# A balanced-experts router and its FFN: each full expert's list, rows, weights and matmuls moved into the rounds that follow

## The chip, the cores and the metric

One core of one Trainium2 chip. The time is the device time of one execution in microseconds (us); lower is better. The kernel before took 676.96 us (median of 4 runs beside the changed kernel; 678.58 in the 3 runs that the prediction had).

Engines: PE is TensorE's matmuls, PEld its weight loads, DVE VectorE, ACT ScalarE, POOL GpSimd, SP SyncE (it issues DMA).

## The reference, cut to what matters

Linear attention with gates over 4 x 8 x 768 x 48 gives 3072 tokens of 384 numbers. A router then sends every token to one of 8 experts, each with room for exactly 384:

```python
logits = x @ w_gate
order = np.argsort(-logits.flatten())
for idx in order:                       # greedy, best logit first
    tok, e = idx // E, idx % E
    if assigned[tok] >= 0 or counts[e] >= cap: continue
    assigned[tok] = e; counts[e] += 1
for e in range(E):
    h = np.maximum(x[assigned == e] @ w1[e], 0.0)     # 384x384 by 384x1024
    out[assigned == e] = h @ w2[e]                    # 384x1024 by 1024x384
```

## The kernel before

Both kernels do the greedy loop in seven rounds and a last choice. In a round each free token names its best open expert; a search over the key's bits (two searches of four steps) finds the level at which the first expert fills up; tokens above it are assigned for good. So each round fills at least one expert. One search step of the kernel before:

```python
for shift in (12, 8, 4, 0):
    level = steps * unit + base                                 # DVE, 15 levels
    above = cand >= level                                       # DVE, 128 x 24 x 15
    for c in range(NT):                                         # PE, 24 small matmuls
        nc.tensor.matmul(out=cnt[0:NTH, 0:E], lhsT=above[:, c, :], rhs=choice[:, :, c], ...)
    fills = cnt >= wanted; filled = max(fills)                  # DVE
    nc.tensor.matmul(out=digit[:, 0:1], lhsT=ones[0:NTH, :], rhs=filled[0:NTH, :], ...)
    base = digit * unit + base                                  # DVE
```

(Shortened: operand details are left out.) Every line needs the one before it. After the last round one list of all tokens in expert order is made, and then, expert by expert, rows are gathered, turned, and multiplied:

```python
xTs = {0: gather(0)}
for e in range(E):
    if e + 1 < E:
        xTs[e + 1] = gather(e + 1)          # indirect DMA, 3 x 3 transposes, DVE copy
    ffn(e, xTs.pop(e), *weights[e])         # 24 + 24 fp32 products of 128 x 128 by 128 x 384
    if len(weights) < E:
        weights.append(load_weights(len(weights)))   # the first three loaded during attention
```

## Time and profile before

| stage of the profiled run (span 675.2 us) | from, to (us) | what limits it |
|---|---|---|
| attention | 0 to 181 | PE (busy 161 us) and the engines around it |
| router, seven rounds of 29.3 us | 181 to 388 | a chain DVE, PE, DVE, PE; PE busy 28% |
| last choice, list, first gather | 388 to 412 | DVE (busy 11.7 of the first 14 us), then POOL and DMA (POOL busy 6.8 of the last 10) |
| eight FFNs of 31.9 us | 412 to 669 | PE, without a gap (busy 256 of 257 us from 412 to 669) |
| last write | 669 to 675 | |

The lines behind the table are in the prediction. Read it as two stages with opposite limits, one after the other: the router leaves PE mostly idle (28% busy), the FFN leaves DVE, ACT and POOL mostly idle (11 to 15% busy).

### The profile page before, as it was taken

How to read it: one execution, taken by the hardware profiler on the slowest of the kernel's cores; microseconds unless marked ns; L12 is line 12 of the kernel's file. 1: busy time of each engine (PE TensorE's matmuls, PEld its weight loads, DVE VectorE, ACT ScalarE, POOL GpSimd, SP SyncE). 2: the span in 40 equal slices, each digit the busy share in tenths (PEclk: the TensorE clock that was granted, in tenths of full speed). 3: DMA queues.
4: the chain of work that ended last, by engine and by line, in shares of the span. 5: the costliest groups of instructions: out<-in, count | busy, mean ns of one | idle time of the engine just before them, and what ended most of it. 6: DMA issues, size and time to landing. Idle time of an engine off the chain costs nothing.

```text
span 675.2 us, 13443 instructions
## 1 busy us (share of the span) xinstructions
PE 481.7 (71%) x5769; PEld 332.5 (49%) x5769; DVE 274.6 (41%) x827; ACT 101.9 (15%) x245; POOL 104.9 (16%) x173
## 2 busy tenths in 40 slices
PE   2999999999332323223232307999999999999996
PEld 1788878888321312212131204565656565665553
DVE  3566656556457476675757662010101010201010
ACT  3355545442000000000000000010101010101100
POOL 5134343232000000000000006020212121010101
PEclk9999999998755555555555556999999999999999
DMA  8888889891000000000000005242424343300000
GB/s 169 172 185 171 184 172 255 245 345 64 30 2 0 2 0 1 1 1 1 1 1 1 1 0 140 106 151 106 151 105 153 116 141 116 106 23 12 36 0 35
DMA packets 118353, 59.14 MB, mean 88 GB/s; under 512 B 101648, under 2 KB 112912, under 8 KB 118288
## 3 DMA queue, kind: packets, MB, share of 16 engines
q1 hardware_dynamic: 111760, 44.06, 25.3%
q0 software_dynamic: 3072, 9.44, 3.9%
q10 hardware_dynamic: 3456, 4.72, 1.9%
q8 instruction: 47, 0.77, 0.5%
q14 instruction: 18, 0.15, 0.1%
HBM read 48.77 MB, written 9.44 MB: 86 GB/s over the span
## 4 chain that ended last, share of the span: by engine, by line
PE 29%; DVE 22%; issue 19%; POOL 2%; DMA 0%; POOLq 0%; DVEq 0%
PE H L663 10%; PE O L674 9%; PE cnt L507 7%; DVE above L499 4%; POOL out_dram L678 2%; DVE level L496 2%; PE digit L515 1%; DVE best L461 1%; DVE fills L510 1%; DVE filled L513 1%; DVE base L522 1%; PE Xe L651 1%; POOL xe L646 1%; DVE chosen L481 1%; DVE rank_incl L530 1%
## 5 line engine op out<-in xcount | busy, mean ns | idle before, releaser
L507 PE MATMUL cnt<-choice,above 128*15 128x8 bf16 x1344 | 44.5, 175 | 119.2 <-DVE above L499 119.2
L663 PE MATMUL H<-xeT,w 128*128 128x384 f32 x384 | 126.2, 489 | 0.0
L674 PE MATMUL O<-w,hT 128*128 128x384 f32 x384 | 125.2, 486 | 0.0
L507 PEld LDWEIGHTS <-above 128*15 128x15 bf16 x1344 | 38.6, 91 | 146.1 <-DVE above L499 133.7
L674 PEld LDWEIGHTS O<-w,hT 128*128 128x128 f32 x384 | 73.1, 190 | 50.7
L663 PEld LDWEIGHTS H<-xeT,w 128*128 128x128 f32 x384 | 73.2, 192 | 49.4 <-issue 0.9
L668 DVE TENSOR_SCALAR hT<-H 128x384 f32<-128x384 f32 x32 | 17.9, 558 | 120.8 <-PE H L663 105.3
L666 ACT ACTIVATE hT<-H 128x384 f32<-128x384 f32 x32 | 15.7, 490 | 339.7 <-PE H L663 339.7
L646 POOL DMA_INDIRECT xe<-xd,token x24 | 23.3, 971 | 259.2 <-issue 242.2
L678 POOL DMA_INDIRECT out_dram<-o,token x24 | 23.5, 981 | 198.5 <-ACT o L677 197.3
L653 DVE COPY xeT<-Xe 128x384 f32<-128x384 f32 x24 | 12.3, 553 | 100.4 <-PE Xe L651 98.4
L225 DVE COPY_PREDICATED am<-mask,A 128x512 f32<-128x512 int32 x48 | 32.4, 729 | 34.8 <-PE A L220 34.8
L151 PE MATMUL L<-g,wcum 128*128 128x384 f32 x48 | 24.3, 593 | 10.0 <-POOL ramp_i L402 10.0
L677 ACT COPY o<-O 128x384 f32<-128x384 f32 x24 | 11.5, 478 | 128.1 <-PE O L674 128.1
L499 DVE TENSOR_TENSOR above<-hi,level 128x360 bf16<-128x360 f32 x56 | 29.8, 532 | 1.2
L175 POOL TENSOR_TENSOR kg<-k,ek 128x384 f32<-128x384 f32 x24 | 25.6, 1066 | 27.2 <-ACT ek L163 21.4
L510 DVE TENSOR_TENSOR fills<-cnt,wanted 15x8 f32<-15x8 f32 x56 | 8.6, 153 | 50.0 <-PE cnt L507 50.0
L237 PE MATMUL Y<-v,am 128*64 128x48 f32 x768 | 27.8, 226 | 0.0
L220 PE MATMUL A<-qT,kT 48*64 48x128 f32 x768 | 27.7, 285 | 0.0
L237 PEld LDWEIGHTS Y<-v,am 128*64 128x64 f32 x768 | 24.7, 139 | 3.9 <-issue 3.7
L515 PE MATMUL digit<-filled,ones 15*128 15x1 bf16 x56 | 9.0, 161 | 24.1 <-DVE filled L513 24.1
L160 DVE TENSOR_SCALAR dl<-L 128x384 f32<-128x384 f32 x24 | 13.4, 558 | 27.7 <-PE L L155 27.7
(155 smaller groups left out, 553.3 us busy)
## 6 DMA issues: line engine op xcount, KB each, us to landing
w<-in_moe_w_dram SPq DMA_DIRECT2D x16, 1536.0 KB, 8.2
f<-in_f_logit_dram SPq DMA_DIRECT2D x24, 192.0 KB, 4.2
q<-in_q_dram SPq DMA_DIRECT2D x24, 192.0 KB, 3.9
k<-in_k_dram SPq DMA_DIRECT2D x24, 192.0 KB, 4.0
v<-in_v_dram SPq DMA_DIRECT2D x24, 192.0 KB, 4.2
xd<-x ACTq DMA_DIRECT2D x24, 192.0 KB, 3.6
xe<-xd,token POOLq DMA_INDIRECT x24
out_dram<-o,token POOLq DMA_INDIRECT x24
```

Of the source, the lines that this page charges most:

```text
L151: nc.tensor.matmul(out=Lv, lhsT=wcum[:], rhs=g[:, :, 0:DH], start=True, stop=True)
L175: nc.gpsimd.tensor_tensor(out=kg[:, :, 0:DH], in0=G["k"][:], in1=ek[:], op=ALU.mult)
L220: nc.tensor.matmul(out=A[par][HC * j:HC * j + HC, 128 * hp:128 * hp + 128], lhsT=G["kT"][rows, hp, HC * j:HC * j + HC], rhs=G["qT"][rows, ...
L225: nc.vector.copy_predicated(am[:, par], mask[:].unsqueeze(1).to_broadcast((128, HP, 128)), A[par][:].rearrange("s (a t) -> s a t", t=128))
L237: nc.tensor.matmul(out=Y[par][HC * j:HC * j + HC, DH * hp:DH * hp + DH], lhsT=G["am"][:, par, hp, HC * j:HC * j + HC], rhs=G["v"][:, 2 * h ...
L499: nc.vector.tensor_tensor(out=above[:], in0=cand[:].rearrange("p (c o) -> p c o", o=1).to_broadcast((128, NT, NTH)), in1=level[:].rearrang ...
L507: nc.tensor.matmul(out=cnt[0:NTH, 0:E], lhsT=above[:, c, :], rhs=choice[:, :, c], start=(c == 0), stop=(c == NT - 1))
L646: nc.gpsimd.indirect_dma_start(out=xe[:], out_offset=None, in_=xd[:, :], in_offset=bass.IndirectOffsetOnAxis(ap=token[:, t:t + 1], axis=0))
L663: nc.tensor.matmul(out=Hp[:, 0:CAP], lhsT=w1[:, d, 128 * ft:128 * ft + 128], rhs=xT[:, d, :], start=(d == 0), stop=(d == DC - 1))
L668: nc.vector.tensor_scalar(out=hT[:, ft, :], in0=Hp[:, 0:CAP], scalar1=0.0, scalar2=None, op0=ALU.max)
L674: nc.tensor.matmul(out=O[:, 0:D], lhsT=hT[:, ft, 128 * i:128 * i + 128], rhs=w2[:, ft, :], start=(ft == 0), stop=(ft == FC - 1))
L678: nc.gpsimd.indirect_dma_start(out=outs[t][:, :], out_offset=bass.IndirectOffsetOnAxis(ap=token[:, t:t + 1], axis=0), in_=o[:], in_offset= ...
```

## The change

Its intent is to run the two stages at once. An expert that a round has filled will never change, so its list, its row gather, its weight load and its FFN can start, and its products ("pieces" below: one fp32 product, or the three transposes that turn one block of rows) can be laid into PE's waits in the later rounds. Two queues hold the work, and the router takes from them at fixed places. The core of the diff (cuts marked):

```diff
     def search(choice, over, between):
         for shift in (12, 8, 4, 0):
             above = rt([NT, NTH], "above", BF16)
             tt(above[:], col(over[:], NTH), row(steps[shift][:], NTH), ALU.is_ge)
+            some(pe_work, between[0])          # pieces before cnt
             r = bank("cnt", "r")
             for c in range(NT):
                 nc.tensor.matmul(out=r[0:NTH, 0:E], lhsT=above[:, c, :], rhs=choice[:, c, :], ...)
+            some(dve_work, 2)                  # two bits of the list
             ...fills, filled...
+            some(pe_work, between[1])          # pieces before the digit
             nc.tensor.matmul(out=r[:, E:E + 1], lhsT=units[shift][0:NTH, :], ...)
+            some(dve_work, 1)
             new = rt([NT], "over")
             tt(new[:], over[:], r[:, E:E + 1].to_broadcast((128, NT)), ALU.add)
     ...
     def assign(choice, over, between):
         ...three matmuls of sums...
+        some(pe_work, between[2])
         ...
+    for rnd in range(E - 1):
+        choice, best = choices()
+        high, low = keys(best)
+        over = search(choice, high, (0, 0) if rnd < 2 else (2, 1))
+        stt(over[:], over[:], 65536.0, low[:], ALU.mult, ALU.add)
+        over = search(choice, over, (2, 1))
+        some(dve_work, len(dve_work))
+        assign(choice, over, (0, 0, 10))
+        dve_work.extend(expert_list())         # its last bit extends pe_work by ffn(L)
+        if rnd in (0, E - 2):
+            some(dve_work, len(dve_work))
+    ...last choice, last list...
+    some(pe_work, len(pe_work))                # what is left: the tail
```

Besides, the search keeps over (the key less the level) in place of a level, the logits are stored with the experts innermost, keys are made for the best logit only, ScalarE takes all evacuations of the FFN, and no weights are loaded during attention, because which expert comes first isn't known then.

## The prediction

> **What bounds the kernel now.** I read the windows first, then the page's slices, then the timeline of one search step. By TensorE's clock and the engines' work the span falls into attention (0 to 181 us), router (181 to 388), list and first gather (388 to 412), expert FFNs (412 to 669) and a 6 us end. Windows over the last three stages (length, busy time of each engine, granted clock, DMA share, GB/s):
>
> ```profile
> 181.00:388.00 207.00, 58.79 (x1421) 46.42 (x1422) 132.60 (x523) 0.00 (x0) 0.00 (x0) 0.50 0.00 1
> 388.00:412.00 24.00, 5.46 (x40) 3.49 (x40) 14.12 (x30) 0.00 (x0) 6.84 (x7) 0.50 0.17 45
> 412.00:669.00 257.00, 256.08 (x828) 153.13 (x827) 27.89 (x52) 27.12 (x56) 39.03 (x41) 0.99 0.27 93
> ```
>
> No engine is full in the router: PE 28%, DVE 64%, ACT, POOL and DMA idle. It is latency, a chain that goes back and forth. In the FFN stage PE is full. The change wants to lay the second stage's matmuls into the first's holes. One search step of the timeline (start, length, engine, line):
>
> ```profile
> 230.09 0.79 PE L507 MATMUL cnt<-choice,above 128*15 128x8 bf16 x24 [1.09 <-DVE above L499]
> 230.81 0.10 PEld L515 LDWEIGHTS <-ones 15*128 15x128 bf16 x1
> 230.92 0.15 DVE L510 TENSOR_TENSOR fills<-cnt,wanted 15x8 f32<-15x8 f32 x1 [0.89 <-PE cnt L507]
> 231.11 0.15 DVE L513 TENSOR_REDUCE filled<-fills 15x1 bf16<-15x8 f32 x1
> 231.32 0.16 PE L515 MATMUL digit<-filled,ones 15*128 15x1 bf16 x1 [0.43 <-DVE filled L513]
> 231.51 0.16 DVE L522 SCALAR_TENSOR_TENSOR base<-digit,base 128x1 f32<-128x1 f32 x1 [0.25 <-PE digit L515]
> 231.71 0.23 DVE L496 TENSOR_SCALAR level<-steps,base 128x15 f32<-128x15 f32 x1
> 231.97 0.53 DVE L499 TENSOR_TENSOR above<-hi,level 128x360 bf16<-128x360 f32 x1
> ```
>
> A step takes 2.47 us (the next cnt starts at 232.56), and PE has two holes in it: 0.43 us before digit and 1.09 before cnt. Eight steps make 19.8 of a round; successive choices start 29.3 us apart (chain of waits: best at 271.05, 300.34, 329.61), so 9.5 us are the assignment and the new choice, nearly all DVE. From the page, what is to fill the holes, and the clock:
>
> ```profile
> L663 PE MATMUL H<-xeT,w 128*128 128x384 f32 x384 | 126.2, 489 | 0.0
> L674 PE MATMUL O<-w,hT 128*128 128x384 f32 x384 | 125.2, 486 | 0.0
> ...
> PEclk9999999998755555555555556999999999999999
> ```
>
> The loops give 8 x 24 products of each kind, the page counts 384: an fp32 product is two passes, each 126.2/384 = 0.33 us of PE. The chain of waits shows 48 of them in 15.48 us. So one of the change's pieces (one product) costs **0.645 us** at full clock, and a piece that turns rows (three transposes) 0.33 (9 in 0.98 us). An expert is 3 x 0.33 + 48 x 0.645 = 31.9 us. A piece is bigger than the hole before digit, and two (1.29) are bigger than the hole before cnt. This decides the case.
>
> [...] 0.50 in the router, 0.99 in the FFN, with the rise about 2.5 us after dense matmuls begin at 413.5. But the windows show 0.50 at 150 to 155 us with PE busy throughout, after a stretch of tiny matmuls and a 0.70 us gap, so "busy" in the trace isn't all that counts. [...] the trace has 617 for the old layout with experts outermost and 358 for count, whose inner axis is contiguous. The new layout makes the inner axis contiguous, so I take 0.36.
>
> **The change part by part.**
>
> *Cheaper steps.* level (0.23 + 0.03 gap) goes; base on one column becomes over on 24 (+0.02). A step with no pieces: 2.47 - 0.26 + 0.02 = 2.23 us.
>
> *Cheaper choice.* The two products for high and low and their reduces go (2 x 0.27 + 2 x 0.53 by start-to-start); six key operations on 24 elements come (four before the search, 0.8). Choices: four operations at 0.39, two reduces at 0.39, one of 0.2: 2.6. With keys and above (0.57): 4.0 us to the first cnt.
>
> *Assignment.* About the same number of DVE operations: 1.4 until the sums are on PE, then some 4.9 = 6.3.
>
> *Step with pieces (two, then one).* PE: 2 x 0.645, cnt 0.80, then one piece beside fills and filled (0.645 against 0.43), digit 0.16, and some 0.1 of handover: 3.0 us. The DVE half (over, above: 0.8) lies under the two pieces.
>
> *Ten pieces after the sums.* 6.45 us; the sums end at 1.4, so PE is free at 7.9 and, with the next two pieces, at 9.2. DVE reaches cnt at 6.3 + 4.0 = 10.3, so these ten are wholly hidden.
>
> *The list.* index 6 x 0.19 = 1.1, members 0.36 + 0.4, place 0.4 and one matmul, lines 0.95, number 0.75, in_line 6 x 0.69 = 4.1, tokens 1.1 on PE (24 matmuls took 1.12) and 0.4: 10.2 us alone. Spread over four steps as 2 + 1 bits each, some 1.4 to 1.8 us of DVE meets 1.2 us of slack in a step: I take 0.6 late in each of three steps and 1.5 in the one with tokens: 3.3 us.
>
> *Removed at the end.* The list of 388 to 402 and the wait for the gather until 412; and the prefetch of three experts' weights in attention. The 16 weight loads took 8.2 us to landing (median). In the new kernel an expert's loads start with its list, over 10 us before its first piece, so I expect no wait, nor from the rows: issue is about 1.3 us for each of three gathers and 3 us of DMA, under the next search.
>
> *Sum, in us from the start.* Router begins at 181.2 (the branch before it stays).
> Round 0: 4.0 + 7 x 2.23 + 1.4 = 21.0, to 202.2; assignment 6.3 and the whole list 10.2, to 218.7.
> Round 1: 4.0, four steps without pieces 8.9, three with 9.0, the last one's end 1.9, to 242.5; 3 more for warming, to 245.5.
> Rounds 2 to 6: 10.3 + 7 x 3.0 + 1.9 + 3.3 = 36.5, less where bits overlap; I take 36 each, 180, to 425.5. A round is so 7 us **longer** than before.
> Then assignment 6.3 and list 10.2, the last choice 2.9, another list 10.2, and no piece under them but the ten: 29.6, to 455.
> Pieces done by then: 22 in round 1 and 34 in each of five rounds, 192 of 8 x 51 = 408. Left: 12 products and four experts, 7.7 + 4 x 31.9 = 135.4, and 2.5 for a cold start: 593. End 6.6 as before: span 600. The measured time lies 2 to 3 us above the span: **602 us**, 11% less than 678.6.
>
> As a cross-check: 192 pieces hidden are 3 x 31.9 + 3 x 0.33 + 36 x 0.645 = 120 us of FFN; the router pays about 37 back by longer rounds, the first list and the warming; the list and gather stage is a few us longer than its 24, as there are two lists. 120 - 37 - 6 = 77, and 678.6 - 77 = 602.
>
> **The rivals.** *The clock stays at half while pieces and cnt alternate.* A piece is then 1.29 us, a step with pieces near 5.0: 44 such steps (4 in round 1, 8 in each of five) x 2.0 = 88 us worse, about 690, no gain. For it: the drop at 150 us with PE busy. Against: 1.94 of 3.0 us are dense full-array passes, at half clock 3.87 of 5, denser than attention, which keeps 1.00 most of the time. Some drops are likely, the wholly cold case is not (4%). *PE has slack and the steps stay DVE-bound.* That would be so if a product were one pass of 0.33 us: rounds near 29, span near 555. Against it: the count of 384. *Rows or weights come late[...],* as weights can no longer be prefetched and an expert isn't known before it is full: some 5 us for each of the first two experts, 610. *The saving is all from the cheaper chain, the pieces add what they hide:* seven rounds at 25 and nothing hidden would give about 650; against it is PE's 28% in the router.
>
> **The range and the chances.** The uncertain terms are the handover in 44 filled steps (0.2 each way: 9 us), the clock (0 to +30), the list's lateness (+-8) and the choice's reduces (+-4). More of this points up than down, and one thing down is a faster attention end without 9.4 MB of weight loads. Range 575 to 635. Faster by over 2% (under 665): 0.95; within 2%: 0.03; slower: 0.02.
>
> **What would show it.** Steps with pieces of about 3.0 us in rounds 2 to 6 at a clock of 1.00, cnt following two pieces at once with above long done; steps of 2.23 in round 0; rounds of about 36 us; reduces of 0.36 us; an FFN tail without gaps of about 138 us after some 25 us of poor PE use. Wrong would be a clock near 0.5 in rounds 2 to 6 (pieces of 1.29), PE waiting on xe or weights, steps where cnt waits on DVE, or a tail much over 140.

Where passages are marked as cut, they stated rules of the hardware that no trace of this case shows. No term of the sum is cut: it came to a span of 600 us and a time of 602. Of what stands between the cuts, 0.50 and 0.99 are TensorE's granted clock in the windows quoted there, and 617 and 358 are ns of a tensor_reduce over 192 elements. Three things rested on the cut passages:

- That a piece laid before cnt delays cnt was not shown before the change. The changed kernel shows it: above ends at 289.15, cnt starts at 289.79, when the two pieces before it are through.
- The prices of DVE operations at sizes new to the kernel (such as 0.19 us with the gap at 24 elements, 0.69 at 512) were worked out by a rule. The trace of the kernel before has fp32 tensor_tensors of 183 ns at 24 elements (L545), 357 at 192 (L481), 532 at 360 (L499) and 758 at 576 (L621); straight lines between these points give 233 at 72 and 691 at 512 (estimate), the same prices. The changed kernel measured 179 to 183 ns at 24, 226 and 243 at 72 and 682 at 512.
- The 3 us for warming in round 1 and the 2.5 for a cold start are estimates. The trace of the kernel before shows what they stand for: dense products begin at 413.69, and the clock is 0.50 until 415, 0.61 in the next us and 1.00 from 416.

## The result, and the profile after

595.89 us median (592.44 to 598.83, 4 runs) against 676.96 of the kernel before (4 runs): ratio 0.8795, 95% interval 0.8722 to 0.8867. Ratios here are the mean time of one kernel's fast runs over that of the other's in the same rounds, so not quite the ratio of the medians quoted. The prediction said 602, 575 to 635. The profiled run has a span of 590.6 us.

Windows of the changed kernel over rounds 2 to 6, the last two lists, and the tail (start:end, length, then PE, PEld, DVE, ACT and POOL busy, the granted clock, DMA share, GB/s):

```profile
237.00:272.00 35.00, 32.89 (x309) 18.59 (x305) 23.24 (x91) 3.90 (x8) 4.83 (x5) 1.00 0.34 114
272.00:307.00 35.00, 32.21 (x301) 18.47 (x301) 23.45 (x93) 5.55 (x12) 3.86 (x4) 1.00 0.34 119
307.00:343.00 36.00, 32.75 (x274) 18.32 (x273) 23.07 (x90) 3.76 (x8) 5.85 (x6) 0.91 0.35 121
343.00:381.00 38.00, 35.89 (x325) 19.84 (x323) 23.53 (x93) 3.90 (x8) 4.84 (x5) 0.96 0.32 109
381.00:416.00 35.00, 32.19 (x301) 18.32 (x300) 23.25 (x91) 5.55 (x12) 3.86 (x4) 1.00 0.33 114
416.00:441.40 25.40, 10.49 (x72) 6.21 (x72) 22.34 (x79) 0.48 (x1) 4.05 (x4) 0.70 0.62 216
441.40:584.10 142.70, 139.43 (x448) 82.56 (x448) 0.33 (x2) 26.61 (x58) 15.47 (x16) 0.98 0.10 34
```

PE went from 28% busy in the router to over 90% in these rounds, and the clock from 0.50 to 0.91 to 1.00. A round is longer than before (35 to 38 us against 29.3), as predicted. In the last-lists window PE is busy only 10.5 of 25.4 us: a hole that the change leaves. One filled search step, from the timeline (start, length, engine, line, operation):

```profile
287.35 0.91 PE L694 MATMUL H<-xeT,w 128*128 128x384 f32 x2
287.46 0.15 DVE L446 TENSOR_TENSOR fills<-cnt,wanted 15x8 f32<-15x8 f32 x1
287.65 0.15 DVE L456 TENSOR_REDUCE filled<-fills 15x1 bf16<-15x8 f32 x1
287.72 0.67 DVE L446 TENSOR_TENSOR in_line<-line,ramp 128x512 bf16<-128x512 f32 x1
288.20 0.17 PE L528 MATMUL cnt<-filled,unit 15*128 15x1 bf16 x1
288.30 1.56 PE L694 MATMUL H<-xeT,w 128*128 128x384 f32 x4
288.40 0.18 DVE L446 TENSOR_TENSOR over<-over,cnt 128x24 f32<-128x24 f32 x1
288.62 0.53 DVE L446 TENSOR_TENSOR above<-over,steps 128x360 bf16<-128x360 f32 x1
289.07 1.28 DVE L446 TENSOR_TENSOR in_line<-line,ramp 128x512 bf16<-128x512 f32 x2
289.79 0.75 PE L520 MATMUL cnt<-choice,above 128*15 128x8 bf16 x24
```

The line with x2 is one piece, the line with x4 two. above ends at 289.15, but cnt starts at 289.79, when the two pieces before it are through: PE sets the step now, not DVE. The next step's piece begins at 290.46, 3.11 us after the first line. In round 0, which has no pieces, cnt starts at 184.19 and 186.37 in the chain of waits: 2.18 us. So three pieces (1.94 us) lengthen a step by 0.94 and are half hidden.

In the tail PE stops once per expert. The timeline of PE between two experts (in the bracket: idle before it and what ended it):

```profile
484.82 1.15 PE L683 MATMUL Xe<-ident,xe 128*128 128x128 f32 x9
486.74 15.75 PE L694 MATMUL H<-xeT,w 128*128 128x384 f32 x48 [0.78 <-ACT xeT L686]
```

### The profile page after: what moved, and what is told of

Read it like the earlier page. It is cut to its first block, busy times and chain, and to the rows that moved or that the text cites. A ratio compares the mean times of both kernels' runs of the same rounds, so it can differ in the third digit from the quotient of the medians.

```text
span 590.6 us, 13979 instructions
## 1 busy us (share of the span) xinstructions
PE 497.5 (84%) x5943; PEld 325.2 (55%) x5943; DVE 273.4 (46%) x903; ACT 127.6 (22%) x301; POOL 106.2 (18%) x184
## 3 DMA queue, kind: packets, MB, share of 16 engines
q0 software_dynamic: 3072, 9.44, 4.8%
## 4 chain that ended last, share of the span: by engine, by line
PE 25%; issue 24%; DVE 18%; POOL 3%; POOLq 0%; ACT 0%; DVEq 0%
PE H L694 9%; PE O L705 7%; PE cnt L520 6%; POOL out_dram L710 2%; DVE above L446 2%; DVE masked L446 1%; DVE in_line L446 1%; PE cnt L528 1%; DVE tcopy L446 1%; PE tokens L650 1%; DVE incl L555 1%; DVE rank L446 1%; DVE over L446 1%; DVE best L456 0%; DVE pick L456 0%
## 5 line engine op out<-in xcount | busy, mean ns | idle before, releaser
L694 PE MATMUL H<-xeT,w 128*128 128x384 f32 x384 | 141.8, 512 | 5.6 <-ACT xeT L686 5.6
L705 PE MATMUL O<-w,hT 128*128 128x384 f32 x384 | 139.2, 508 | 0.0
L694 PEld LDWEIGHTS H<-xeT,w 128*128 128x128 f32 x384 | 70.2, 194 | 46.3 <-ACT xeT L686 6.6
L520 PEld LDWEIGHTS <-above 128*15 128x15 bf16 x1344 | 36.5, 88 | 59.5 <-DVE above L446 30.6
L520 PE MATMUL cnt<-choice,above 128*15 128x8 bf16 x1344 | 42.1, 166 | 27.8 <-DVE above L446 27.8
L698 ACT ACTIVATE hT<-H 128x384 f32<-128x384 f32 x64 | 31.4, 491 | 139.4 <-PE H L694 139.4
L149 PE MATMUL L<-g,wcum 128*128 128x384 f32 x48 | 22.8, 559 | 10.5 <-ACT g L142 10.5
L446 DVE TENSOR_TENSOR in_line<-line,ramp 128x512 bf16<-128x512 f32 x48 | 30.6, 682 | 0.0
L446 DVE TENSOR_TENSOR above<-over,steps 128x360 bf16<-128x360 f32 x49 | 26.1, 533 | 1.7
L686 ACT COPY xeT<-Xe 128x384 f32<-128x384 f32 x24 | 10.3, 493 | 58.6 <-PE Xe L683 58.4
L153 PEld LDWEIGHTS L<-ind,g 128*64 128x64 f32 x384 | 13.5, 141 | 14.0 <-issue 12.9
```

The source lines that it names most:

```text
L149: nc.tensor.matmul(out=Lv, lhsT=wcum[:], rhs=g[:, :, 0:DH], start=True, stop=True)
L446: nc.vector.tensor_tensor(out=out_, in0=a, in1=b, op=op)
L520: nc.tensor.matmul(out=r[0:NTH, 0:E], lhsT=above[:, c, :], rhs=choice[:, c, :], start=(c == 0), stop=(c == NT - 1))
L694: nc.tensor.matmul(out=L["H"][:, 0:CAP], lhsT=L["w1"][:, d, 128 * ft:128 * ft + 128], rhs=xT[:, d, :], start=(d == 0), stop=(d == DC - 1))
L698: nc.scalar.activation(out=hT[:, ft, :], in_=L["H"][:, 0:CAP], func=AF.Relu)
L705: nc.tensor.matmul(out=L["O"][:, 0:D], lhsT=hT[:, ft, 128 * i:128 * i + 128], rhs=L["w2"][:, ft, :], start=(ft == 0), stop=(ft == FC - 1))
```

## The experiments

All kernels told of gave the right result. Times are medians; each stands beside the kernel before on the same chip (673.7 to 674.2 us there). The comparisons between variants also lean on each one's profiled run.

**none: no piece laid in any round.** Does the gain come from the overlap, or from the cheaper search and the shorter attention? Two buffers are larger.

```diff
-    search(choice, high, (0, 0) if rnd < 2 else (2, 1)) ... (2, 1) ... assign(choice, over, (0, 0, 10))
+    search(choice, high, (0, 0)) ... (0, 0) ... assign(choice, over, (0, 0, 0))
-    e = rt([1], "e", I32)          xe: bufs=9
+    e = rt([1], "e", I32, E)       xe: bufs=21
```

> No piece is laid in a round; all 408 come after the last list (buffers for the rows are more, so that nothing blocks). Theory (the gain is the FFN matmuls that lie under the router): router rounds 2 to 6 fall from 35.9 to about 31 us (steps of 2.18 us plus some 4.5 us of list that no longer hides), the tail grows from 142 to about 258 us, in all about 679 us, as slow as the kernel before. Rival (the cheaper search and the shorter attention give the gain, the pieces add what they hide): about 600 us or under 650.

685.97 us, ratio to before 1.017 (1.013 to 1.021): slower than the kernel before. From the first assignment to the last (first and last start of sure, the tile of the tokens that a round assigns) the router took 187.4 us, against 219.4 in the changed kernel, and the tail 267.6 against 142.7. So the 192 pieces in the rounds cost the router 32 us and save the tail 125. The lines of sure in this run and in the changed kernel (min/median/max in ns, first to last start):

```profile
L453 DVE SCALAR_TENSOR_TENSOR sure<-over,choice x7: 357/358/359, 196.9 to 384.3; 128x192 bf16<-128x192 f32 x7
```

```profile
L453 DVE SCALAR_TENSOR_TENSOR sure<-over,choice x7: 357/357/359, 196.9 to 416.3; 128x192 bf16<-128x192 f32 x7
```

Its windows in rounds 3 and 4:

```profile
272.00:307.00 35.00, 10.82 (x278) 8.71 (x279) 26.98 (x115) 0.00 (x0) 3.00 (x3) 0.50 0.36 119
307.00:343.00 36.00, 10.79 (x278) 8.59 (x278) 28.22 (x108) 0.00 (x0) 2.99 (x3) 0.50 0.27 94
```

PE is as idle as before and the clock is 0.50 again. The rival is out: the whole gain, and a little more, is the overlap; the rest of the change costs more than it returns. Where, the two profiled runs show: attention ends 5.7 us earlier (175.4 against 181.1), the router and the eight lists take 4.0 us more until the first product (at 412.0 against 413.7), and the products take 9.9 us more (264.7 against 254.8). Most of the last is that the experts follow each other every 32.99 us in place of 31.95: each waits for the copy of its turned rows (0.73 to 0.78 us of idle PE), which the kernel before makes one expert ahead.

**gap10: pieces only after the sums.** The ten pieces in the assignment's gap stay, those in the search steps go (with the buffers of the run above).

> Only the ten pieces after the sums stay, none in the search steps. Theory: they are wholly hidden, 60 pieces x 0.645 = 39 us off the run without pieces, about 641 us; rounds no longer than in that run (about 31 us). The 132 pieces in the steps, which lengthen the steps from 2.18 to 3.12 us, are then worth about 45 us net. Rival (pieces in the steps cost the router what they save in the tail): about 596 us, as the changed kernel.

650.66 us, ratio 0.964 (0.960 to 0.968), 35 us under the run without pieces where 39 were expected. The rounds took 187.8 us, the same as the 187.4 without any piece: these ten are wholly hidden, as the prediction had it.

```profile
L453 DVE SCALAR_TENSOR_TENSOR sure<-over,choice x7: 357/357/357, 198.0 to 385.8; 128x192 bf16<-128x192 f32 x7
```

The other 55 us of the gain come from the pieces in the steps, though each of those lengthens its step.

**oneone: one piece before cnt, not two.** Only that number changes (and the larger e).

> One piece before cnt instead of two, one before digit as before. Theory (with two and one PE is full in the step, so a piece taken out shortens the step by a piece, 3.12 to about 2.47 us, and comes back in the tail): 28 us more tail, 25 less router, some 4 us of list work that shows: about 602 us, within 2% of the changed kernel. Rival (the pieces lie in holes and are free): step stays near 3.1 us, 28 us slower, about 624.

621.79 us (616.72 to 625.71), ratio 0.923. The theory failed here: 602 was expected, and the rival's 624 is what came. But the rival's reason is wrong too. Where the clock is 1.00 the step did shrink by a piece: cnt starts at 260.56, 263.10, 265.63, 268.17 in the timeline, 2.54 us apart. The windows show what happened elsewhere, in the same columns as above:

```profile
388.00:392.00 4.00, 4.00 (x30) 1.75 (x29) 2.80 (x14) 0.49 (x1) 0.00 (x0) 0.50 0.96 375
392.00:396.00 4.00, 4.00 (x30) 1.76 (x29) 2.86 (x8) 0.00 (x0) 0.00 (x0) 0.50 1.06 379
396.00:400.00 4.00, 4.00 (x54) 2.01 (x52) 1.66 (x5) 0.49 (x1) 0.00 (x0) 0.50 0.04 10
400.00:404.00 4.00, 4.00 (x33) 1.80 (x30) 1.49 (x8) 0.00 (x0) 2.17 (x3) 0.50 0.17 49
404.00:408.00 4.00, 4.00 (x30) 1.80 (x31) 1.07 (x5) 0.00 (x0) 0.66 (x1) 0.54 0.35 102
381.00:418.00 37.00, 34.26 (x279) 16.93 (x278) 22.49 (x89) 2.44 (x5) 3.83 (x4) 0.72 0.31 107
```

For nearly 20 us TensorE ran at half clock, with PE busy all the time. There a pair of matmuls takes 1.65 us in place of 0.91 and a step nearly 4 us. Over rounds 2 to 6 the window clocks are 0.90, 0.80, 0.91, 0.87 and 0.72. From one sure to the next these rounds took 32.2, 35.8, 34.1, 35.3 and 37.8 us; had all taken 32.2, the run would be some 14 us shorter, so the half clock is most of the 20 us that the theory missed (an estimate from this one profile). The reading, not yet shown: with fewer dense matmuls in the mix the clock drops for longer. A new theory, then: pieces do two things, they fill waits and they keep the clock up.

**dummy: the piece taken out is replaced by useless work.** A test of that: the kernel above, plus one fp32 product of a piece's size on constants before cnt in each filled step. The edit does a little more than that: between[0] is also set in the second search of round 0, which has no pieces, so 48 useless products are laid and not 44 (96 matmul instructions in the trace).

```diff
             r = bank("cnt", "r")
+            if between[0]:
+                nc.tensor.matmul(out=r[:, 64:64 + D], lhsT=ident[:], rhs=junk[:], start=True, stop=True)
```

> The run with one piece before cnt and one before digit, plus one useless fp32 product of a piece's size before cnt in each filled step. If that run was slow because its sparser PE lets the clock fall: the useless product keeps the clock at or near 1.00, steps are 3.12 us as in the changed kernel, rounds too, the tail is 28 us longer, in all about 624 us, hardly slower than without the useless work (621.8). Rival (something else in that order is slow, list work that shows): the useless products add their 44 x 0.65 = 28 us, about 650.

632.26 us (628.92 to 634.61), ratio 0.937. The useless products, 31 us of PE at full clock, cost 10.5. Their line in the trace:

```profile
L521 PE MATMUL cnt<-junk,ident x96: 486/486/1009, 189.7 to 425.9; 128*128 128x384 f32 x96
```

Its windows in rounds 2 to 6 have clocks of 0.92, 0.95, 0.91, 0.96 and 1.00; the last, in place of 0.72:

```profile
381.00:418.00 37.00, 33.99 (x318) 19.10 (x315) 23.21 (x91) 3.92 (x8) 4.14 (x5) 1.00 0.31 103
```

That is nearer to the clock theory's 624 than to the rival's 650. That the useless work raised the clock is shown: the windows say so, and over the whole run the mean granted clock is 0.915 to 0.925 in all four runs, against 0.861 to 0.884 in the four without it. How much time came back that way is not separated, because part of the useless work also lies in waits that were there anyway: at full clock, four steps with list work take 12.2 us without it (oneone, cnt from 349.88) and 13.6 with it (cnt from 330.79), so it costs 0.35 us in each and not 0.645. Of the 8 us over 624, the four products in round 0 account for 2.5 (steps of 2.85 in place of 2.18 us, at half clock); half-clock stretches that remain (0.92 and 0.95 in rounds 2 and 3, where the changed kernel has 1.00) may be the rest.

**threeone: three pieces before cnt.** The other direction.

```diff
-    (2, 1)
+    (3, 1)
```

> Three pieces before cnt, one before digit. Theory (PE is the bound in filled steps at full clock, so a further piece only moves from tail to step): step 3.76 us, rounds 5 us longer, tail 28 us shorter, and the clock no longer falls in rounds 4 and 5: 590 to 596 us. Rival (the pieces lengthen the step's chain by more than themselves): over 600.

592.80 us (592.68 to 595.05), ratio 0.8808 (0.8767 to 0.8849), no different from the changed kernel's 0.8795. cnt starts 3.76 us apart, the rounds take 246.8 us (199.2 to 446.0), 27.4 more than in the changed kernel, for 44 pieces of 0.645 = 28.4 less in the tail. With PE the bound and the clock up (0.922 to 0.931 over the run), it made no difference here where these pieces lay.

**nofetch and nofetch2: the kernel before without prefetch.** In the changed kernel the router began at 175.4 us, not at 181.1. Is that the missing weight loads? In the first try the three loads were written after the list instead of into attention's loop.

> The kernel before, with the first three experts' weights loaded after attention, not during it. Theory (the weight loads are why attention ends 5.8 us earlier in the changed kernel): router starts near 175.5 us instead of 181.1, total about 671 us, nothing lost later because the loads lie under the router. Rival (the new layout and pools shortened attention): router starts at 181, total 677.

674.73 us, ratio 1.0005 (0.993 to 1.008): inconclusive, as the loads were still issued from 100 to 135 us; the scheduler had moved them up. So the weights' pool was moved into the room that attention frees:

```diff
-    wpool = ctx.enter_context(tc.tile_pool(name="weights", bufs=3))      # at the top
...
+    wpool = ctx.enter_context(tc.tile_pool(name="weights", bufs=3))      # after attention
...
+    weights = [load_weights(e) for e in range(3)]
     xTs = {0: gather(0)}
```

> The run without prefetch again, since in the first try the weight loads were still issued during attention (the scheduler moved them up): now the weights' buffers lie in the room that attention frees, so no load can start before it ends. Theory (the weight loads delay the end of attention): router starts near 175.5 us as in the changed kernel, total about 671 us or 5 to 6 below the kernel before. Rival (layout and pools): router starts at 181, total as before.

The router's first DVE instruction, in this run and in the kernel before:

```profile
175.86 0.26 DVE L432 TENSOR_SCALAR sign<-logits 128x192 int32<-128x192 int32 x1 [4.68 <-SPq L372]
```

```profile
181.14 0.26 DVE L434 TENSOR_SCALAR sign<-logits 128x192 int32<-128x192 int32 x1 [5.02 <-SPq L375]
```

5.3 us earlier in the profiled runs; the median is 671.27 against 674.24, ratio 0.9961 (0.9927 to 0.9996). So this edit does shorten attention, by 5 us in the traces and 3 in the times of many runs. In the kernel before, the window from 145 to 155 us, with the loads under way (338 GB/s), is at a mean clock of 0.73; in this run the same window is at 1.00 (24 GB/s). That fits the weight loads as the cause; but the edit also moves the weights' pool, and no run tells the two apart.

**gap12, endfill, best: the holes that are left.** If PE is what counts, the waits it still has can be read from the trace: 0.95 to 1.10 us before the first cnt of rounds 2 to 6, and 15 of the 25 us of the last two lists. gap12 lays 12 pieces after the sums; endfill lays eight pieces before and eight after the token matmuls of the last two lists; best does both.

```diff
-            assign(choice, over, (0, 0, 10))
+            assign(choice, over, (0, 0, 12))                     # gap12, best
...
+        def list_among(n):                                       # endfill, best
+            while dve_work:
+                bit = dve_work.popleft()
+                if bit.__name__ == "tokens": some(pe_work, n)
+                bit()
+                if bit.__name__ == "tokens": some(pe_work, n)
-        some(dve_work, len(dve_work))                            # after round 6 and at the end
+        list_among(8)
```

> Twelve pieces after the sums, not ten. Theory: PE waits 1.0 to 1.6 us for above at the end of that gap in each round, which two pieces (1.29 us) fill: rounds as long as before, 6 rounds x 1 to 1.29 us less tail, about 6 us faster, 590 us. Rival (the gap is set by DVE and its wait is only apparent, the two pieces delay the first cnt): no change, 596.

> Eight pieces before and eight after the token matmuls of the last two lists, where the changed kernel has PE idle (some 15 of 25 us between 416 and 441 us). Theory: up to 24 of the tail's pieces go under the lists, 15.5 us less tail and 2 us less of half clock, 2 us of delay of the lists: about 15 us faster, 581 us. Rival (the last lists are only late because of PE, so that laying pieces there delays them as much): no change.

> Both: twelve pieces in the gap and the last lists filled. Theory: the two holes are apart, so the gains add: about 21 us faster than the changed kernel, 575 us. Rival: as one alone, 581 to 590.

587.05, 584.47 and 569.54 us; ratios 0.8713, 0.8667 and 0.8455 (all within 0.004 of that). Against the changed kernel, by the ratios and by the medians, gap12 gained 6 to 9 us, endfill 9 to 11 of the expected 15, and best 23 to 26, where 21 were expected. endfill's profiled router took 229.7 us (196.0 to 425.7) where the changed kernel's took 219.4; the code there is the same in both kernels. Of these 10 us, one stall in round 4 makes up 3: DVE (fills) and ScalarE (the copy of turned rows) both stand 4.5 us, until 339.7, for a cause that the trace gives only as "remote", and one step takes 7.88 us where the changed kernel's takes 4.66. The rest goes with clocks of 0.86 and 0.95 in places. In best, where the gap is full, the same windows stay at 1.00, 1.00, 1.00, 1.00 and 0.95, and so they do in gap12. That the fuller gap is what holds the clock up in these two is argued from these windows; the clock also varies from run to run.

**best2: the next expert's rows turned early.** The changed kernel's tail shows 0.78 us of PE idle per expert, waiting for ScalarE's copy of the turned rows (lines above).

```diff
-            pe_work.extend(ffn(L))
+            bits, last = ffn(L), []
+            while pe_work and len(last) < 4:
+                last.insert(0, pe_work.pop())
+            pe_work.extend(bits[:TE] + last + bits[TE:])
```

> The run with twelve pieces and filled last lists, and the three turns of an expert's rows laid before the last four products of the expert before it. PE waits some 0.8 us at each expert for ScalarE's copy of the turned rows; laid ahead, that copy is hidden: about 7 x 0.8 = 5 us faster than 569.5, 564 us. Rival (rows land too late for that, PE then waits on the gather): no change or slower.

566.90 us (564.63 to 570.01, 6 runs), ratio 0.8411 (0.8373 to 0.8449). The row turns in the tail are 31.94 us apart (461.39, 493.33, 525.28) where they were 32.99 apart in the changed kernel. The gain against best is 2.6 us by the medians (5 were expected) and the two intervals overlap, so only the tail's saving is shown, not the total's. This is the fastest version here: 16% under the kernel before and some 4 to 5% under the changed one (both ratios to the kernel before, 0.8411 over 0.8795). They were run at other times.

## Why the prediction was right

The point, 602, was 6 us above the median, with the mechanism as told: pieces under the router make PE the bound of a step, and the longer rounds are paid back several times in the tail. That the point came so close is in part luck, as misses of both signs cancel (14 us too high in all, 5 too low). Term by term, on the profiled run (span 590.6 against 600 predicted):

| step of the sum | predicted | measured | difference |
|---|---|---|---|
| router begins | 181.2 | 175.4 | -5.8 |
| round 0 | 21.0 | 21.5 | +0.5 |
| its assignment and list, to the first cnt of round 1 | 20.5 | 18.6 | -1.9 |
| rest of round 1 | 22.8 | 23.0 | +0.2 |
| rounds 2 to 6 | 180 | 177.8 | -2.2 |
| last lists | 29.6 | 25.2 | -4.4 |
| tail | 137.9 | 142.5 | +4.6 |
| end | 6.6 | 6.6 | 0 |

- **A piece costs 0.645 us and is bigger than the hole** stands. The prediction called it two passes; the trace shows two matmul instructions of 0.32 us each.
- **Step 2.23 without and 3.0 with pieces**: 2.18 and 3.12. The handover was put at 0.1 and is about 0.2. **PE becomes the bound of the step** is shown by cnt starting late after above, and by the steps of 2.54, 3.12 and 3.76 us with one, two and three pieces before cnt.
- **The ten pieces are wholly hidden**: shown by gap10, whose rounds are as long as without pieces.
- **The list comes 3.3 us late per round**: about 1.1 us in round 3 (steps of 3.64, 3.12, 3.11 and 3.71 us). It was over-sized because its bits run while PE still works off pieces. An undisturbed round took 34.7 us, not 36; that the five together came within 2.2 us of the 180 is luck, as half-clock stretches in rounds 4 and 5 and a wait for turned rows in round 4 (37.6 and 36.0 us) took up that room.
- **The start of the router** was named as something that could go down but was left in the sum as it was; it was the largest miss, and nofetch2 points to the missing weight loads as the cause.
- **The last lists** were over-sized by 4.4 us, as they were put at 10.2 us each, with the token matmuls after the whole list. The trace shows six groups of token matmuls, each starting as soon as its part of in_line is ready.
- **The tail** was under-sized by 4.6 us. The turns had been priced at their 0.98 us of PE; the wait for ScalarE's copy, which the kernel before hides by turning one expert ahead, was left out. It is 0.78 us for each of the four whole experts in it, and their turns are 32.99 us apart where 31.9 was priced, which for four makes up nearly all of the 4.6. The cold start was priced rightly: the first 12 products took 10.4 us, against 7.7 + 2.5.
- **The rivals.** Half clock throughout did not happen here, but the oneone run shows how near it is: one piece fewer per step and the clock falls to 0.72 in a round. The prediction's 4% was about all rounds at half clock; it didn't see that the number of pieces itself bears on this. Late rows or weights: no wait of PE on a DMA shows in these rounds. "The saving is all from the cheaper chain" is refuted by the run without pieces, at 1.017 of the kernel before.

## What to carry to other kernels

Where a latency-bound stage with an idle PE precedes a PE-bound one, lay the second's matmuls into the first even if they don't fit its holes: here 192 pieces cost the chain 32 us and saved 125. Once PE was the bound of the filled stage, it made no difference here where a piece lay (threeone 592.8 us against 595.9), so look next for the places where PE still waits (the gap before a round, the last lists, a copy not made ahead). And fill densely: with one piece fewer among the tiny matmuls of each step the clock here was 0.50 for nearly 20 us of one round, and the run cost more than the shorter step saved (oneone: 621.8 us against 595.9).

## What else the traces show

- A busy PE did not always have the full clock. It stayed at 0.50 for nearly 20 us with the PE row busy 4.00 of 4.00 us (oneone, 388 to 408 us), and in the kernel before at 150 to 155 us with PE busy 5.00 of 5.00. With eight useless products laid among the tiny ones of the last round its clock was 1.00 in place of 0.72. At which density of work it drops, no run shows.
- The layout that a tensor_reduce reads. The same reduce of 192 fp32 elements to 24 took 617 ns with the reduced axis strided by 24 elements and 353 ns with it contiguous; the first line is from the groups of the kernel before, the second from the tile best of the changed one (min/median/max):

```profile
L461 DVE TENSOR_REDUCE best<-masked 128x24 f32<-128x192 f32 x16 | 9.9, 617 | 0.3
```

```profile
L456 DVE TENSOR_REDUCE best<-masked x8: 353/353/354, 176.0 to 431.0; 128x24 f32<-128x192 f32 x8
```

- The order in which a tensor_tensor reads. An fp32 tensor_tensor took 357 ns at 192 elements, 532 at 360 and 3350 at 3072 (in_row) in the kernel before. One whose first operand is read across its rows took longer: adding tcopy (read in transposed order from SBUF) to sums in PSUM took 610 ns at 192 elements, where the add in the kernel before, with both in one order, took 353:

```profile
L446 DVE TENSOR_TENSOR rank<-tcopy,sums x7: 607/610/612, 200.8 to 420.1; 128x192 f32<-128x192 f32 x7
```

The strided reads of these two took 617 - 353 = 264 and 610 - 353 = 257 ns more for 192 elements, 1.4 and 1.3 ns for each (an estimate from these two differences).
